# Retention attention and a low-rank mixer on one core: the third batch's k loaded and turned ahead of its q, and another order for the second batch's steps

## Chip, cores and metric

One core of one Trainium2 chip. The metric is the device time of one execution of the kernel in microseconds. The median of three runs before the change is 323.8 us (321.01 to 323.85).

## What is computed

The reference takes q, k and v (8 batches, 8 heads, 576 tokens, 64 channels) and four weight matrices. Cut to what matters:

```python
scores = scale * np.matmul(q, k.transpose(0, 1, 3, 2))
Dmat = np.where(rel >= 0, gamma[:, None, None] ** rel[None, :, :], 0.0)
attn = np.matmul(scores * Dmat[None], v)              # gamma = 1 - 2**(-5-head), rel = row - column
x = attn.transpose(0, 2, 1, 3).reshape(B, S, H * D)   # 8 x 576 x 512
h = x.transpose(0, 2, 1) @ U @ V                      # rank 32, over the tokens
u = x + h.transpose(0, 2, 1)
out = u + np.maximum(u @ w_ch1, 0.0) @ w_ch2          # 512 -> 2048 -> 512
```

## The kernel before

**Stages.** The 8 x 576 tokens make nine groups of 512 tokens for the MLP (j = 0 to 8). Attention and mixer work batch by batch. The first two batches (b = 0 and 1) run ahead of everything else in `early`; batch b = 2 runs inside the MLP units of group j = 1, and every later batch b inside group j = b - 1. All data are computed in bf16; a matmul accumulates in a PSUM bank, and another engine copies it out.

**The order in `early`.** The instructions of each engine run in the order in which the program issues them. For batches 0 and 1 that order stands in the string `EARLY` (lines 33 to 63), a list of steps separated by semicolons. `step` (line 631) issues the instructions of one step: the first number after the name is the batch, the second is the pair of heads, hp = 0 to 3, and what follows are the numbers of the PSUM banks that the step writes or the engine that does it. The names that are needed here, for a pair of heads of batch 1:

- `tk`, `tq`: PE turns k and q (transposes into a bank). `ck`: ACT copies the turned k into one of the two halves of `kvT` (`kT_bufs`, line 167). `qs`: DVE scales the turned q into `qz`.
- `sc`: PE forms the scores, into three banks. `ma`, `mb`, `ml`: DVE masks them into `ret`.
- `vs`: DVE scales v (from `v_given`, which lies in `kv_runs`) into `v_all`. `st`: PE sums the states, k times v. `S`: copies them out.
- `it`: PE multiplies the masked scores with v; `nt` adds the last block and q times the state. `xa`, `xb`: the result is copied into `x_t`.
- `dn`, `at`, `ux`, `uv`, `ua`, `ub`: the mixer and the turning of its sum u into `uT_t`.
- `M n`: PE runs unit n of the MLP of group 0, four matmuls of 128x512. Units 16 to 31 are the second product, four for each block of 128 tokens. They depend on nothing that batch 1 makes, and stand between its steps as filler. `O i`: DVE adds u to block i, and SP issues its store. `Y`, `Q`: the first three units of group 1, whose input is all of batch 1's u.
- `kt c`: SP issues a turn by DMA (`turn_by_dma`, line 475) of blocks c and c + 1 of batch 2's k, from `k_sets[2]` into `kT_sets`. `kT_sets[0]` is a tile of its own (`kT_all`), `kT_sets[1]` is the whole of `kvT`.

**Loads.** POOL issues the loads that convert from float32. In the step `hv` (`load_second_kv`, line 252) SP first loads parts of batch 1's k and all but one block of its v as float32; POOL casts the k of pairs 0 and 1 into `k_sets[1]`, scales one block of v, and calls `load_batch(2)` (line 304): four loads of q, then five blocks of k, then five of v. After `early` POOL issues `load_batch(3)`, with a scaling of v between the loads, and batch 3's q.

**Batches 2 and later.** `attention_steps` (line 560) puts steps at places among the MLP units. For b = 2 PE turns q (`psq`), k comes turned from `kT_sets`; DVE scales v (`scale_v`); `visit` runs state sums (`pss`), scores (`sc`), masks and the running state (`S`). From b = 3 on q and k are both turned by DMA, each batch's during the batch before it. Before the change batch b's k goes to `kT_sets[(b - NTURN) % 2]` with `NTURN` = 3, and batch 2's to `kT_sets[1]`, that is `kvT`, which batch 1's scores read until `sc 1 3`.

Of the kernel before, what the change touches and what calls it, by code (L numbers as in the profile page):

```python
# [14 lines left out]
class Pinned:  # L15
# [15 lines left out]


EARLY = """
    w 9; vs 0 1 POOL; lg; lw 0; lw 1; lw 2; lw 3; tk 0 0 0; w 4 4; tq 0 0 1; qs 0 0; ck
    0 0; bk 0 0 2; w 3 0; sc 0 0; vs 0 0 DVE; tk 0 1 3; mb 0 0; kk 0 0; ck 0 1; w 1 1;
    tq 0 1 4; st 0 0 0; ma 0 0; gv 0 2; it 0 0 1 2; qs 0 1; ml 0 0; S 0 0 ACT; bk 0 1 3;
    vl 0; gv 0 3; sc 0 1; exp 3; nt 0 0; mb 0 1; ma 0 1; kk 0 1; tk 0 2 4; tq 0 2 0; ml
    0 1; xa 0 0 ACT; qs 0 2; ck 0 2; tk 0 3 3; st 0 1 1; sc 0 2; S 0 1 ACT; it 0 1 4 0;
    ma 0 2; ck 0 3; mb 0 2; nt 0 1; tq 0 3 1; xb 0 0 ACT; bk 0 3 3; xa 0 1 ACT; bk 0 2
    2; ux 0 0 4; kk 0 2; xb 0 1 DVE; w 1 0; dn 0 0 0; ml 0 2; at 0 0 ACT; dn 0 1 2; at 0  # L40
    1 ACT; qs 0 3; vs 0 3 DVE; sc 0 3; vs 0 2 POOL; lw 4; lw 5; lw 6; lw 7; zm; l2; hk;
    st 0 2 1; kk 0 3; uv 0 0; ml 0 3; ma 0 3; mb 0 3; it 0 2 0 2; S 0 2 ACT; ua 0 0 ACT;
    st 0 3 3; nt 0 2; it 0 3 1 4; S 0 3 ACT; ux 0 1 3; xa 0 2 DVE; nt 0 3; xb 0 3 DVE;
    xb 0 2 ACT; dn 0 2 0; y 0 0; uv 0 1; xa 0 3 ACT; y 1 0; ux 0 2 2; at 0 2 DVE; y 2 0;
    dn 0 3 1; uv 0 2; ua 0 1 ACT; ux 0 3 4 0; at 0 3 ACT; ua 0 2 DVE; y 0 1; uv 0 3; y 1
    1; y 2 1; y 0 2; y 1 2; y 2 2; ub 0 3 DVE; ua 0 3 ACT; y 0 3; R 0; y 1 3; y 2 3; hu
    4 4; hu 2 0; R 1; ha 4; hu 1 2; hu 0 1; hu 3 3; R 2; M 3; ha 1; ha 2; M 4; R 3; z 3;
    exv; misc; hv; M 5; R 4; M 6; R 5; M 7; R 6; M 8; ha 0; R 7; ha 3; M 9; R 8; M 10; R
    9; M 11; R 10; M 12; R 11; M 13; R 12; M 14; R 13; M 15; R 14; M 16; R 15; M 17; M
    18; M 19; M 20; M 21; tq 1 0 0; qs 1 0; M 22; tk 1 0 1; tq 1 1 2; qs 1 1; ck 1 0; tk  # L50
    1 2 3; sc 1 0 4 0 1; M 23; mb 1 0; ml 1 0; tk 1 1 2; ma 1 0; vs 1 1 DVE; ck 1 2; ck
    1 1; M 24; tk 1 3 0; sc 1 1 3 1 4; M 25; M 26; ck 1 3; vs 1 0 DVE; st 1 1 2; ml 1 1; st 1
    0 4; S 1 1 ACT; ma 1 1; S 1 0 ACT; it 1 0 0 3; mb 1 1; it 1 1 2 1; nt 1 0; nt 1 1;
    vs 1 2 DVE; st 1 2 4; xa 1 0 ACT; xa 1 1 ACT; vs 1 3 DVE; xb 1 1 DVE; tq 1 2 0; tq 1
    3 2; xb 1 0 DVE; st 1 3 1; qs 1 2; qs 1 3; S 1 2 ACT; dn 1 0 4; O 0; sc 1 2 3
    0 2; at 1 0 DVE; mb 1 2; ml 1 2; S 1 3 ACT; ma 1 2; dn 1 1 1; M 27; sc 1 3 4 0 2; kt 0; kt 2; kt 4; M
    28; ux 1 1 3; at 1 1 ACT; ml 1 3; ma 1 3; mb 1 3; it 1 2 1 2; uv 1 1; M 29; it 1 3 4
    0; nt 1 2; ua 1 1 ACT; xb 1 2 DVE; O 1; nt 1 3; ux 1 0 3; xa 1 2 ACT; dn 1 2 1; xa 1
    3 ACT; at 1 2 DVE; uv 1 0; ux 1 2 2; xb 1 3 ACT; dn 1 3 4; uv 1 2; ua 1 0 ACT; O 2;
    at 1 3 DVE; ux 1 3 0 1; M 30; uv 1 3; ua 1 2 ACT; ua 1 3 ACT; ub 1 3 DVE; M 31; Y 0  # L60
    0; Y 0 1; Y 0 2; Y 0 3; Q 0; O 3; Y 2 0; Y 2 1; Y 2 2; Y 2 3; Q 2; Y 1 0; Y 1 1; Y 1
    2; Y 1 3; Q 1
"""


# [1 line left out]
def kernel(  # L67
# [72 lines left out]
    NRUNS = 3  # L140
    NTURN = 3
# [162 lines left out]
    def load_batch(b, blocks=range(NB)):  # L304

        if b < NRUNS:
            for hp in range(NHP):
                load_runs(in_runs(q_raw[b % NQ]), q, b, hp)
        elif blocks[0] == 0:
            m, pad = (NB - 1, slice(HALF, P)) if b % 2 == 0 else (0, slice(0, HALF))  # L310
            for x in (k_sets, v_sets):
                pool.memset(x[b % NSET][pad, m, :, :], 0.0)
        if b < NRUNS:
            for x, src in ((k_sets, k), (v_sets, v)):
                for m in blocks:
# [52 lines left out]
    def att_transposes(b, hp, st):  # L368
        if b < NRUNS:
            psq = turn_runs_by_head(in_runs(q_raw[b % NQ]), hp, "psq")  # L370
        elif b < NTURN:
            psq = turn_blocks(in_blocks(q_raw[b % NQ]), hp, "psq")
        else:
            psq = qT_sets[(b - NTURN) % 2][:, :, hp, :]
        st["qT"] = q_by_chunks(b, hp, psq)
        st["kT"] = kT_sets[(b - NTURN) % 2][:, :, hp, :]


    def q_by_chunks(b, hp, psq):
# [180 lines left out]
    def attention_steps(b, at, gap, at_mixer, at_turn=2):  # L560

        if b // 2 not in pairs:
            new_pair(b)
        pair = pairs[b // 2]
        x_t = work.tile([P, NB, dm], BF16, tag="x_t", name="x_t")
        sts = [{} for _ in range(NHP)]
        mst = {}
        steps = []

        for hp in range(NHP):  # L570
            if b < NRUNS:
# [25 lines left out]
    def early(mlp, mlp1, between):  # L597
# [33 lines left out]
        def step(op, args):  # L631
# [55 lines left out]
            if op == "lg":  # L687
                x = in_runs(k_raw)[:, H - 1, 0, 0:1]
# [25 lines left out]
            st, h, cols = sts[b, n], slice(2 * n, 2 * n + 2), slice(n * P, (n + 1) * P)  # L714
# [126 lines left out]
            elif op == "ux":  # L841
                k = (NB - 1) // len(i)
# [13 lines left out]
            elif op == "uv":  # L856
                k = (NB - 1) // len(st["u"])
# [19 lines left out]
        st = {"at": at_sb}  # L877
# [376 lines left out]
    while n < SP:  # L1254
        m = min(n, SP - n)
# [141 lines left out]
```

## Time and profile before

| | us |
|---|---|
| median of three runs | 323.8 |
| the three runs | 321.01, 323.80, 323.85 |
| the profiled execution's own time | 322.16 |
| its span, first to last instruction | 320.4 |
| PE busy | 310.9 |
| DVE busy | 231.4 |
| POOL busy | 158.9 |
| ACT busy | 149.5 |

The profiled execution's own time is 1.8 us longer than the span of its instructions. The granted TensorE clock is 1.00 throughout. PE, DVE, ACT, POOL and SP are TensorE, VectorE, ScalarE, GpSimd and SyncE; PEld is the weight load, which overlaps PE. A row of the profile names the output tile and the inputs, the shape, the number of instructions and, in brackets, the idle time of the engine before it with what ended it. All helpers record one line number, L25, so groups are told apart by their tiles: `ps_b` is a bank of `early`, `ps_y` the MLP, `pss` and `sc` the later batches' state sums and scores.

### The profile page before, as it was taken

The page shows a single profiled execution, that of the slowest core. Times are in us where ns is not written, and L with a number is a line of the kernel's source. Part 1 is how long each engine was busy: PE and PEld are TensorE (multiplying, and loading weights), DVE is VectorE, ACT ScalarE, POOL GpSimd, SP SyncE. Part 2 cuts the span into 40 slices and gives each one's busy share as a digit, 9 for nine tenths or more (in the row PEclk, how much of TensorE's full clock was granted, in tenths as well). Part 3 has the DMA queues.
Part 4 walks back from the last instruction along what each step waited for, and adds up shares of the span by engine and source line. Part 5 has one row for each costly group of instructions (what it writes and reads, how often), then busy time and mean ns, then how long its engine had stood idle before and what let it go on. Part 6 is the DMA issues. An engine that isn't in the chain of part 4 may idle for free.

```text
span 320.4 us, 9737 instructions
## 1 busy us (share of the span) xinstructions
PE 310.9 (97%) x4120; PEld 205.9 (64%) x4120; DVE 231.4 (72%) x552; ACT 149.5 (47%) x305; POOL 158.9 (50%) x197
## 2 busy tenths in 40 slices
PE   8999999999999999999999999999999999999995
PEld 3664446644544677845788878556867784585484
DVE  5977537749898998789878978897889772352244
ACT  7667523347620674067406750675067506604610
POOL 8582339948940998399649914650400040040040
PEclk9999999999999999999999999999999999999999
DMA  8999999999998999999999996994420043002003
GB/s 123 189 200 206 200 200 134 170 182 148 139 154 203 90 143 146 159 188 151 144 207 126 167 118 85 170 152 85 127 72 4 3 96 120 0 32 101 0 2 132
DMA packets 154524, 40.59 MB, mean 127 GB/s; under 512 B 139088, under 2 KB 153456, under 8 KB 154480
## 3 DMA queue, kind: packets, MB, share of 16 engines
q0 software_dynamic: 91344, 17.09, 68.9%
q1 hardware_dynamic: 63136, 22.88, 37.0%
q8 instruction: 32, 0.52, 0.7%
q14 instruction: 12, 0.10, 0.1%
HBM read 36.85 MB, written 9.44 MB: 144 GB/s over the span
## 4 chain that ended last, share of the span: by engine, by line
PE 64%; DVE 24%; DMA 6%; SPq 2%; issue 2%; POOL 0%; ACT 0%; DVEq 0%; POOLq 0%; ACTq 0%
PE ps_y L25 54%; DVE S L25 8%; DVE ret L25 7%; PE ps_b L25 4%; PE xh L25 3%; DMA kvT<-k_all 2%; DMA given<-in_v_dram 2%; DVE y_sums L25 2%; SPq L25 2%; DMA kv_runs<-in_v_dram 2%; DVE o_sb L25 2%; DVE kv_runs L25 1%; DVE u_t L25 1%; PE sc L25 1%; PE ps_h L25 1%
## 5 line engine op out<-in xcount | busy, mean ns | idle before, releaser
L25 PE MATMUL ps_y<-uT_t,w_sb 128*128 128x512 bf16 (+3 forms) x768 | 131.0, 326 | 0.0
L25 ACT ACTIVATE y_t<-ps_y 128x512 bf16<-128x512 f32 x144 | 85.5, 597 | 61.8 <-PE ps_y L25 60.7
L25 PEld LDWEIGHTS <-w_sb 128*128 128x128 bf16 x768 | 68.1, 98 | 50.4
L25 POOL TENSOR_TENSOR o_sb<-o_sb,u_t 128x512 f32<-128x512 f32 (+1 forms) x24 | 24.4, 1034 | 93.2 <-DVE o_sb L25 92.7
L25 PEld LDWEIGHTS <-y_t 128*128 128x128 bf16 x576 | 55.2, 98 | 18.0
L25 PE MATMUL ps_y<-w_sb,y_t 128*128 128x256 bf16 (+1 forms) x352 | 57.7, 311 | 0.0
L25 DVE SCALAR_TENSOR_TENSOR S<-S,keep,pss 128x64 bf16<-128x64 bf16 x168 | 46.9, 279 | 5.1
L25 DVE TENSOR_TENSOR o_sb<-ps_y,o_sb 128x512 f32<-128x512 f32 (+1 forms) x37 | 24.4, 662 | 26.5 <-PE ps_y L25 13.1
L25 DVE TENSOR_TENSOR ret<-sc,qsrow 128x640 bf16<-128x640 f32 x48 | 37.2, 816 | 7.2 <-PE sc L25 3.8
L25 POOL DMA_DIRECT2D k_all<-in_k_dram x36 | 30.9, 861 | 9.2 <-DMA w_sb<-in_moe_w_ch_dram 7.6
L25 PEld LDWEIGHTS <-y_sums 128*128 128x128 bf16 x336 | 32.0, 98 | 5.0
L25 POOL TENSOR_TENSOR v_all<-v_all,vs 128x512 bf16<-128x512 bf16 (+1 forms) x25 | 27.9, 1116 | 9.3 <-DMA v_all<-in_v_dram 8.8
L25 POOL DMA_DIRECT2D q_all<-in_q_dram x37 | 29.0, 796 | 4.2 <-DMA w_sb<-in_moe_w_ch_dram 4.2
L25 DVE TENSOR_TENSOR y_sums<-y_t 128x512 bf16<-128x512 bf16 x28 | 14.2, 508 | 22.1 <-ACT y_t L25 22.1
L25 PE MATMUL ps_y<-w_sb,y_sums 128*128 128x256 bf16 x224 | 27.3, 273 | 0.0
L25 PE MATMUL ps_y<-kv_runs,y_t 128*128 128x256 bf16 x224 | 27.1, 273 | 0.0
L25 POOL DMA_DIRECT2D v_all<-in_v_dram x31 | 26.8, 874 | 0.3 <-DMA q_all<-in_q_dram 0.3
L25 ACT CAST S<-pss 128x64 bf16<-128x64 f32 x24 | 5.1, 210 | 46.8 <-issue 41.4
L25 ACT ACTIVATE x_t<-xh,xs 128x320 bf16<-128x320 f32 x48 | 22.7, 524 | 7.0 <-PE xh L25 5.6
L25 DVE TENSOR_TENSOR u_t<-ps_h,x_t 128x512 bf16<-128x512 f32 (+1 forms) x35 | 22.3, 681 | 0.8 <-PE ps_h L25 0.4
L25 DVE TENSOR_TENSOR y_sums<-y_sums,y_t 128x512 bf16<-128x512 bf16 x28 | 14.2, 508 | 1.0
L25 POOL COPY landed<-uT_t 128x4 bf16<-128x4 bf16 (+1 forms) x4 | 0.8, 190 | 27.8 <-DMA uT_t<-u_t 27.8
(130 smaller groups left out, 313.8 us busy)
## 6 DMA issues: line engine op xcount, KB each, us to landing
out_dram<-o_sb SPq DMA_DIRECT2D x35, 256.0 KB, 2.9
w_sb<-in_moe_w_ch_dram POOLq DMA_DIRECT2D x8, 512.0 KB, 12.2
v_all<-in_v_dram POOLq DMA_DIRECT2D x25, 128.0 KB, 7.3
k_all<-in_k_dram POOLq DMA_DIRECT2D x24, 128.0 KB, 6.3
q_all<-in_q_dram POOLq DMA_DIRECT2D x20, 128.0 KB, 4.5
q_all<-in_q_dram POOLq DMA_DIRECT2D x12, 144.0 KB, 5.8
given<-in_v_dram SPq DMA_DIRECT2D x8, 128.0 KB, 4.2
kv_runs<-in_v_dram SPq DMA_DIRECT2D x3, 256.0 KB, 6.1
```

The source lines that it names most:

```text
L25: return self._tc.keep_in_program_order(call(*args, **kwargs))
```

## The change

In `EARLY` only batch 1's part differs, from `M 22` on. Cut to it, with the unchanged steps ahead of it left out:

```diff
-    ... M 21; tq 1 0 0; qs 1 0; M 22; tk 1 0 1; tq 1 1 2; qs 1 1; ck 1 0; tk
-    1 2 3; sc 1 0 4 0 1; M 23; mb 1 0; ml 1 0; tk 1 1 2; ma 1 0; vs 1 1 DVE; ck 1 2; ck
-    1 1; M 24; tk 1 3 0; sc 1 1 3 1 4; M 25; M 26; ck 1 3; vs 1 0 DVE; st 1 1 2; ml 1 1; st 1
-    0 4; S 1 1 ACT; ma 1 1; S 1 0 ACT; it 1 0 0 3; mb 1 1; it 1 1 2 1; nt 1 0; nt 1 1;
-    vs 1 2 DVE; st 1 2 4; xa 1 0 ACT; xa 1 1 ACT; vs 1 3 DVE; xb 1 1 DVE; tq 1 2 0; tq 1
-    3 2; xb 1 0 DVE; st 1 3 1; qs 1 2; qs 1 3; S 1 2 ACT; dn 1 0 4; O 0; sc 1 2 3
-    0 2; at 1 0 DVE; mb 1 2; ml 1 2; S 1 3 ACT; ma 1 2; dn 1 1 1; M 27; sc 1 3 4 0 2; kt 0; kt 2; kt 4; M
-    28; ux 1 1 3; at 1 1 ACT; ml 1 3; ma 1 3; mb 1 3; it 1 2 1 2; uv 1 1; M 29; it 1 3 4
-    0; nt 1 2; ua 1 1 ACT; xb 1 2 DVE; O 1; nt 1 3; ux 1 0 3; xa 1 2 ACT; dn 1 2 1; xa 1
-    3 ACT; at 1 2 DVE; uv 1 0; ux 1 2 2; xb 1 3 ACT; dn 1 3 4; uv 1 2; ua 1 0 ACT; O 2;
-    at 1 3 DVE; ux 1 3 0 1; M 30; uv 1 3; ua 1 2 ACT; ua 1 3 ACT; ub 1 3 DVE; M 31; Y 0
+    21; M 22; M 23; tq 1 0 0; tq 1 1 1; tk 1 0 2; M 24; tk 1 1 3; ck 1 0; qs 1 0; sc
+    1 0 4 0 2; qs 1 1; ma 1 0; mb 1 0; M 25; ck 1 1; sc 1 1 1 3 4; mb 1 1; M 26; tk
+    1 3 0; tk 1 2 3; ma 1 1; M 27; kt 0; kt 2; kt 4; vs 1 0 DVE; vs 1 1 DVE; ck 1 2;
+    ck 1 3; ml 1 0; st 1 0 1; st 1 1 3; it 1 0 0 2; ml 1 1; S 1 0 ACT; vs 1 3 DVE;
+    it 1 1 4 1; S 1 1 ACT; nt 1 0; nt 1 1; xb 1 0 ACT; xa 1 0 ACT; vs 1 2 DVE; O 0;
+    tq 1 2 3; st 1 2 2; qs 1 2; xb 1 1 ACT; xa 1 1 ACT; S 1 2 DVE; tq 1 3 0; st 1 3
+    1; sc 1 2 3 4 2; qs 1 3; S 1 3 ACT; ma 1 2; ml 1 2; dn 1 1 0; at 1 1 ACT; M 28;
+    sc 1 3 1 0 3; mb 1 2; ma 1 3; M 29; it 1 2 2 4; dn 1 0 1; at 1 0 ACT; mb 1 3; ml
+    1 3; nt 1 2; it 1 3 0 3; ux 1 1 1; nt 1 3; xa 1 2 ACT; uv 1 1; ux 1 0 2; O 2; xb
+    1 2 ACT; dn 1 2 4; xb 1 3 ACT; O 1; ua 1 1 ACT; xa 1 3 DVE; uv 1 0; dn 1 3 3; at
+    1 2 DVE; ux 1 2 0; ua 1 0 DVE; at 1 3 ACT; ux 1 3 1 4; uv 1 2; uv 1 3; M 30; M
+    31; ua 1 3 ACT; ua 1 2 DVE; ub 1 3 DVE; Y 0 0; ...
```

The loads of batch 2, and where turned k goes:

```diff
 def load_batch(b, blocks=range(NB)):
         if b < NRUNS:
+            for m in blocks:
+                load_block(k_sets[b % NSET], k, b, m)
             for hp in range(NHP):
                 load_runs(in_runs(q_raw[b % NQ]), q, b, hp)
-        elif blocks[0] == 0:
+            for m in blocks:
+                load_block(v_sets[b % NSET], v, b, m)
+            return
+        if blocks[0] == 0:
 ...
-        if b < NRUNS:
-            for x, src in ((k_sets, k), (v_sets, v)):
-                for m in blocks:
-                    load_block(x[b % NSET], src, b, m)
-            return
@@ att_transposes
-        st["kT"] = kT_sets[(b - NTURN) % 2][:, :, hp, :]
+        st["kT"] = kT_sets[b % 2][:, :, hp, :]
@@ attention_steps
-                                     (k_sets[(b + 1) % NSET], kT_sets[(b + 1 - NTURN) % 2]))):
+                                     (k_sets[(b + 1) % NSET], kT_sets[(b + 1) % 2]))):
@@ step
             if op == "kt":
-                turn_by_dma(k_sets[2], kT_sets[1], b)
+                turn_by_dma(k_sets[2], kT_sets[0], b)
```

So `M 22` and `M 23` now stand ahead of batch 1's first turn, and `M 27` ahead of its state sums; the masks `ma` and `mb` of pairs 0 and 1 ahead of the scaling of v on DVE; seven of the eight copies into `x_t` on ACT, where it was five; the three turns of batch 2's k ahead of `O 0`'s store on SP's queue, where they stood behind it, and into `kT_all`; and for every batch from 3 on the two buffers of turned k are exchanged.

More of the change, by code (lines that the diff above doesn't have):

```diff
@@ L33 @@
 EARLY = """
[L34 to L50, printed above, removed]
-    1 2 3; sc 1 0 4 0 1; M 23; mb 1 0; ml 1 0; tk 1 1 2; ma 1 0; vs 1 1 DVE; ck 1 2; ck
@@ L58 @@
-    0; nt 1 2; ua 1 1 ACT; xb 1 2 DVE; O 1; nt 1 3; ux 1 0 3; xa 1 2 ACT; dn 1 2 1; xa 1
-    3 ACT; at 1 2 DVE; uv 1 0; ux 1 2 2; xb 1 3 ACT; dn 1 3 4; uv 1 2; ua 1 0 ACT; O 2;
-    at 1 3 DVE; ux 1 3 0 1; M 30; uv 1 3; ua 1 2 ACT; ua 1 3 ACT; ub 1 3 DVE; M 31; Y 0
-    0; Y 0 1; Y 0 2; Y 0 3; Q 0; O 3; Y 2 0; Y 2 1; Y 2 2; Y 2 3; Q 2; Y 1 0; Y 1 1; Y 1
-    2; Y 1 3; Q 1
+    w 9; vs 0 1 POOL; lg; lw 0; lw 1; lw 2; lw 3; tk 0 0 0; w 4 4; tq 0 0 1; qs 0 0;
+    ck 0 0; bk 0 0 2; w 3 0; sc 0 0; vs 0 0 DVE; tk 0 1 3; mb 0 0; kk 0 0; ck 0 1; w
@@ new lines @@
+    1 1; tq 0 1 4; st 0 0 0; ma 0 0; gv 0 2; it 0 0 1 2; qs 0 1; ml 0 0; S 0 0 ACT;
+    bk 0 1 3; vl 0; gv 0 3; sc 0 1; exp 3; nt 0 0; mb 0 1; ma 0 1; kk 0 1; tk 0 2 4;
+    tq 0 2 0; ml 0 1; xa 0 0 ACT; qs 0 2; ck 0 2; tk 0 3 3; st 0 1 1; sc 0 2; S 0 1
+    ACT; it 0 1 4 0; ma 0 2; ck 0 3; mb 0 2; nt 0 1; tq 0 3 1; xb 0 0 ACT; bk 0 3 3;
+    xa 0 1 ACT; bk 0 2 2; ux 0 0 4; kk 0 2; xb 0 1 DVE; w 1 0; dn 0 0 0; ml 0 2; at
+    0 0 ACT; dn 0 1 2; at 0 1 ACT; qs 0 3; vs 0 3 DVE; sc 0 3; vs 0 2 POOL; lw 4; lw
@@ new lines @@
+    5; lw 6; lw 7; zm; l2; hk; st 0 2 1; kk 0 3; uv 0 0; ml 0 3; ma 0 3; mb 0 3; it
+    0 2 0 2; S 0 2 ACT; ua 0 0 ACT; st 0 3 3; nt 0 2; it 0 3 1 4; S 0 3 ACT; ux 0 1
+    3; xa 0 2 DVE; nt 0 3; xb 0 3 DVE; xb 0 2 ACT; dn 0 2 0; y 0 0; uv 0 1; xa 0 3
+    ACT; y 1 0; ux 0 2 2; at 0 2 DVE; y 2 0; dn 0 3 1; uv 0 2; ua 0 1 ACT; ux 0 3 4
+    0; at 0 3 ACT; ua 0 2 DVE; y 0 1; uv 0 3; y 1 1; y 2 1; y 0 2; y 1 2; y 2 2; ub
+    0 3 DVE; ua 0 3 ACT; y 0 3; R 0; y 1 3; y 2 3; hu 4 4; hu 2 0; R 1; ha 4; hu 1
@@ new lines @@
+    2; hu 0 1; hu 3 3; R 2; M 3; ha 1; ha 2; M 4; R 3; z 3; exv; misc; hv; M 5; R 4;
+    M 6; R 5; M 7; R 6; M 8; ha 0; R 7; ha 3; M 9; R 8; M 10; R 9; M 11; R 10; M 12;
+    R 11; M 13; R 12; M 14; R 13; M 15; R 14; M 16; R 15; M 17; M 18; M 19; M 20; M
+    21; M 22; M 23; tq 1 0 0; tq 1 1 1; tk 1 0 2; M 24; tk 1 1 3; ck 1 0; qs 1 0; sc
+    1 0 4 0 2; qs 1 1; ma 1 0; mb 1 0; M 25; ck 1 1; sc 1 1 1 3 4; mb 1 1; M 26; tk
+    1 3 0; tk 1 2 3; ma 1 1; M 27; kt 0; kt 2; kt 4; vs 1 0 DVE; vs 1 1 DVE; ck 1 2;
@@ L63 @@
+    1 2 ACT; dn 1 2 4; xb 1 3 ACT; O 1; ua 1 1 ACT; xa 1 3 DVE; uv 1 0; dn 1 3 3; at
+    1 2 DVE; ux 1 2 0; ua 1 0 DVE; at 1 3 ACT; ux 1 3 1 4; uv 1 2; uv 1 3; M 30; M
+    31; ua 1 3 ACT; ua 1 2 DVE; ub 1 3 DVE; Y 0 0; Y 0 1; Y 0 2; Y 0 3; Q 0; O 3; Y
+    2 0; Y 2 1; Y 2 2; Y 2 3; Q 2; Y 1 0; Y 1 1; Y 1 2; Y 1 3; Q 1
 """
```

## The prediction

> **What bounds the kernel now.** I read the page's busy table first, then the table of waits for who made TensorE (PE) stand idle, first from 42.4 to 71.6 us and then from there to the end.
>
> ```profile
> span 320.4 us, 9737 instructions
> ## 1 busy us (share of the span) xinstructions
> PE 310.9 (97%) x4120; PEld 205.9 (64%) x4120; DVE 231.4 (72%) x552; ACT 149.5 (47%) x305; POOL 158.9 (50%) x197
> ```
>
> ```profile
> PE sc L25 <- DMA kvT<-k_all: 0.7, 1, 0.7
> PE ps_b L25 <- POOL k_all L25: 0.6, 1, 0.6
> PE ps_b L25 <- DVE ret L25: 0.5, 2, 0.3
> PE ps_b L25 <- DVE qz L25: 0.3, 1, 0.3
> ```
>
> ```profile
> PE ps_ut L25 <- DVE u_t L25: 0.3, 1, 0.3
> PE xh L25 <- DVE o_sb L25: 0.2, 1, 0.2
> ```
>
> PE is the bound: 310.9 of 320.4 us. The change adds and removes no arithmetic, so it can win only what PE loses, and of that the stretch in which the second batch (batch 1) runs and batch 2 begins has 2.1 us; all of the 249 us behind it have 0.5. That stretch in PE's order of time (start, length, and in brackets the idle time before):
>
> ```profile
> 42.43 0.45 PE L25 MATMUL ps_b<-ident,q_all 96*64 96x96 bf16 x12
> 42.81 1.04 PE L25 MATMUL ps_y<-w_sb,y_t 128*128 128x512 bf16 x4
> 44.41 0.45 PE L25 MATMUL ps_b<-ident,k_all 128*128 128x128 bf16 x5 [0.57 <-POOL k_all L25]
> ...
> 50.88 0.51 PE L25 MATMUL ps_b<-v_all,k_all 128*64 128x64 bf16 x20
> ...
> 57.60 0.57 PE L25 MATMUL ps_b<-qz,kvT 64*128 64x128 bf16 x10
> 58.10 1.04 PE L25 MATMUL ps_y<-w_sb,y_t 128*128 128x512 bf16 x4
> ...
> 64.48 1.03 PE L25 MATMUL ps_y<-w_sb,y_t 128*128 128x512 bf16 x4
> 65.34 2.75 PE L25 MATMUL ps_y<-uT_t,w_sb 128*128 128x512 bf16 x12
> ...
> 70.23 0.32 PE L25 MATMUL pss<-v_all,k_all 64*64 64x64 bf16 x16
> 70.38 0.30 PE L25 MATMUL sc<-qz,kvT 64*64 64x64 bf16 x16
> 71.34 0.22 PE L25 MATMUL sc<-qz,kvT 64*64 64x64 bf16 x4 [0.66 <-DMA kvT<-k_all]
> ```
>
> The ends shown are modelled and overlap the next start, so I count from start to start. A unit of filler (M n, four matmuls) takes 64.48 to 65.34 = 0.86 us. M 22, at 42.81, was done at 43.67, so the k turn at 44.41 (tk 1 0) lost 0.74 us, not 0.57.
>
> This execution took 322.16 us; the median of the three runs is 323.8 (321.01 to 323.85), 1.64 more. I make the sum against 322.16 and scale it by 323.8/322.16. Less than about 1% a measurement of this kernel cannot tell from no change.
>
> **Part 1: the order of batch 1.** Two things feed it that the order does not move, the casts of k on POOL and the scaling of the landed v on VectorE (DVE):
>
> ```profile
> 43.64 0.72 POOL L25 CAST k_all<-y_sums 128x640 bf16<-128x640 f32 x1 [2.04 <-DMA y_sums<-in_k_dram]
> 44.87 0.72 POOL L25 CAST k_all<-y_sums 128x640 bf16<-128x640 f32 x1 [0.51 <-DMA y_sums<-in_k_dram]
> ```
>
> ```profile
> 50.11 1.29 DVE L25 TENSOR_TENSOR v_all<-kv_runs,vscale 128x512 bf16<-128x512 f32 x2 [2.53 <-DMA kv_runs<-in_v_dram]
> ```
>
> So k is cast at 44.36 (hp 0) and 45.59 (hp 1), and v of the first two pairs is scaled at about 50.75 and 51.40.
>
> In the new order M 22 and M 23 run from 42.43 to 44.15, and both q turns (0.38 each, 42.43 to 42.81) to 44.9. The turn of k hp 0 now comes after its cast and is over at 45.3, M 24 at 46.2, the turn of hp 1 at 46.5, after its cast too. Scores of hp 0 (0.50, 57.60 to 58.10), M 25, scores of hp 1, M 26, the turns for hp 3 and 2 and M 27 bring PE to about 50.7; the copies and masks between these steps lie beside an M each. There it meets the floor of v: the state sums of hp 0 start at about 50.8, where before those of hp 1 started at 50.88.
>
> So at that floor M 27 is done, where before M 26 was the last. From 50.88 to 65.34 were 14.46 us with five units; with four they are 13.60, and from 50.8 PE comes to batch 2's MLP units at 64.4 if the other waits stay as they were: **0.95 us** won.
>
> The waits after the floor are the term I know least. The table marks 0.8 of them (0.5 on ret, 0.3 on qz); start to start, where modelled ends hide part, I read up to 1.5. Walking the new order with the same lengths I find four: v of hp 1, 0.2 (51.4 against 51.2); dn 1 1, whose bank is freed by a q copy queued on DVE behind O 0 and S 1 2, 0.5; it 1 3 for its last mask, 0.25; small ones 0.1. That is 1.05 against 1.5, a gain of 0.4; adding the steps' own lengths alone I end at 63.5, a gain of 0.9. If one bank comes free a DVE operation later than I read it, 0.5 is lost instead. Range -0.5 to 0.9; I take **0.6**, between my two readings. The masks now stand ahead of the v scaling on DVE, which idled 2.53 us there, so nothing is held up by that; the copies of x_t move from DVE to ACT, which was busy 47% of the span.
>
> **Part 2: batch 2's k ahead of its q, and turned at once.** POOL's issues, the k loads' times to landing, the turns on SP's queue with theirs, and the v loads with the median of theirs:
>
> ```profile
> 48.65 2.58 POOL L25 DMA_DIRECT2D q_all<-in_q_dram  x4
> 51.22 4.22 POOL L25 DMA_DIRECT2D k_all<-in_k_dram  x5
> 55.38 4.25 POOL L25 DMA_DIRECT2D v_all<-in_v_dram  x5
> ```
>
> ```profile
> DMA to landing us min/median/max: 5.1/5.5/5.9
> ```
>
> ```profile
> L25 SPq DMA_TRANSPOSE kvT<-k_all x3: 1342/1382/3958, 58.3 to 63.8; - x3
> ...
> DMA to landing us min/median/max: 7.5/8.8/10.2
> ```
>
> ```profile
> v_all<-in_v_dram POOLq DMA_DIRECT2D x4, 128.0 KB, 6.3
> out_dram<-o_sb SPq DMA_DIRECT2D x1, 256.0 KB, 4.6
> v_all<-in_v_dram POOLq DMA_DIRECT2D x1, 64.0 KB, 8.0
> ```
>
> The first turn was issued at 58.3, just after hp 3's scores (57.60 to 58.10) had read kvT for the last time. It now writes kT_all, which nobody reads, and waits for its two k blocks alone. The k issues move up by 2.57 us, so these land at about 54.5, and the turns go out at about 55, 57 and, with the 5.5 us from first to last as before, at most 60.5. With 7.5 to 10.2 to land, the last is there by 68 to 70 and more likely at 68; its chunk was wanted at 70.68 (71.34 less 0.66) and will be at 69.1. The wait goes: **0.7**, and 0 if it stayed.
>
> What this is moved past: O 0's store stands behind the turns on SP's queue, and waits with them; O 0 to O 3 have a buffer each, so nobody waits for that store. q is issued from 52.9 to 55.4, lands by about 61 and is turned on PE after 66. Batch 3's k is turned into kvT, free since 58.2. v is issued at the same times, since the same nine transfers stand before it.
>
> The cover that can go is v's. Its last block, issued at about 58.9, landed 8.0 later, at 66.9, and DVE scaled v at 67.23:
>
> ```profile
> 67.23 1.55 DVE L25 TENSOR_TENSOR v_all<-v_all,vs 128x640 bf16<-128x640 bf16 x2
> 72.03 1.55 DVE L25 TENSOR_TENSOR ret<-sc,qsrow 128x640 bf16<-128x640 f32 x2 [3.25 <-ACT S L25]
> ```
>
> PE's state sums (70.23) need hp 0's half, 0.78 after v. PE 1.55 us earlier wants them at 68.7, so v by 67.9: 1.0 us of room. Of the turns' 13.0 us (58.3 to 71.3) the last 4.4 lay behind v's landing; now that third shares the transfers with v. v comes 0 us later if the transfers have room for both, 2.2 if they share evenly, and that costs PE 0 to 1.2. I charge **-0.3**, nearer to 0: an even share of half of that third already fits the room.
>
> **The sum.** 0.95 + 0.6 + 0.7 - 0.3 = 1.95 us. Behind 72 us PE waits only 0.5 us in all, each time for an engine whose work moves up with PE, and DVE idles 3.25 us before its next block, so I carry the gain to the end: 322.16 - 1.95 = 320.2, which is 321.8 in terms of the median.
>
> **Rivals.** *A, more is won.* The runs at 323.8 may be executions in which the k turns landed 1.64 us later still (their times to landing differ by 2.7). There the removed wait is 1.64 longer, v's charge is not paid, and 1.95 + 1.64 + 0.3 are won: 319.9. For it: that wait is PE's longest in the stretch; against: no trace shows those runs.
>
> *B, v takes the place of kT.* v comes 2.2 late and costs 0.9 more than charged: 1.05 is won, 322.7. For it: room of only 1.0, and v's time to landing, which had grown from 6.3 to 8.0 beside the turns; against: the turns then ran beside batch 3's loads as well.
> The Trainium skill (DMA: Bandwidth & Descriptors, Issuing engines are not separate DMA queues) says that transfers issued by SP and by POOL run on the same 16 engines and interleave, which speaks against turning early and for B. The trace agrees as far as that growth of 1.7 us goes.
>
> *C, slower.* The turns push v behind them altogether, so that v's last block lands at 71.3, where the turns ended before. Scaling hp 0 then ends at 72.1, and the state sums, which without the kT wait could have started at 70.9 before (70.23 + 0.66), start 1.2 us late: 323.4, or 325.0 in the median. It decides from v landing at 70.1, 3.2 later than before. For it: v stands behind k and q in one queue; against: two thirds of the turns delayed v by only 1.7.
>
> **How the numbers follow.** Forecast 0.50, A 0.20, B 0.18, C 0.12. Faster by over 1% (below 320.6): A, and the upper end of the forecast, 0.26. Slower by over 1% (above 327.0): C with 2 us more, 0.05. Within 1%: 0.69. The forecast's own range is 320.6 (0.9 for 0.6, 0.7 and no charge, and the median's scatter) to 323.2 (-0.5 for 0.6, and 0.3 more of charge). To 8 in 10 it takes in B and the larger part of A, and half of C: 319.4 to 324.4.
>
> **What would show it.** No PE wait for POOL's cast; state sums of hp 0 at 50.8; batch 2's first MLP unit near 63.8 instead of 65.34; the turns issued from about 55 and no PE wait for kT; the scaling of v at 67 to 68 and batch 2's state sums near 68.7. It would be wrong if PE stood idle before those sums for v, if the turns were issued no earlier than 58, if the new order held PE more than 1.6 us after 50.8, or if the gain were lost at the start of the third MLP group, where PE reads batch 2's turned u.

## The result, and the profile after

| | before | after |
|---|---|---|
| median, us (20 runs each) | 321.32 | 325.89 |
| lowest and highest, us | 319.60, 323.85 | 322.63, 328.86 |
| ratio to before, 95% interval | | 1.0117 [1.0092, 1.0143] |
| the profiled execution's own time, us | 322.16 | 327.08 |

The ratios are taken over undisturbed runs alone, so they can differ a little from the quotient of the medians. The change made the kernel slower by 1.2%. It was predicted at 321.8 (319.4 to 324.4); the time lies above that range, and a loss came where a gain was forecast. The twenty runs also put the median before at 321.32, not at the 323.8 of the three runs that the forecast was scaled to.

The busy table of after, with its row of the granted clock over the span:

```profile
span 325.4 us, 9740 instructions
PE 311.6 (96%) x4120; PEld 206.2 (63%) x4120; DVE 232.7 (72%) x551; ACT 149.0 (46%) x306; POOL 158.6 (49%) x197
...
PEclk9999999996999999999999999999999999999999
```

PE's work is the same, and the span is 4.94 us longer (325.36 against 320.42). One slice, the tenth (73.2 to 81.4 us), was granted clearly less than the others. The table of waits for PE (us in total, times, longest; its first five rows) names the place:

```profile
PE pss L25 <- DVE v_all L25: 5.2, 1, 5.2
PE ps_warm L25 <- DVE warm L25: 1.1, 1, 1.1
PE ps_b L25 <- POOL v_all L25: 0.6, 1, 0.6
PE ps_y L25 <- DMA uT_t<-u_t: 0.6, 1, 0.6
PE ps_b L25 <- DVE qz L25: 0.3, 1, 0.3
...
```

The waits for `kvT`, for POOL's cast of k and for `ret` are gone. In their place stands one of 5.2 us at batch 2's state sums. (The 0.6 for POOL's `v_all` is at 14.0 us, in batch 0, which the change doesn't touch; from there comes the late start of batch 1 below.) PE's order of time in that stretch:

```profile
64.18 2.75 PE L25 MATMUL ps_y<-uT_t,w_sb 128*128 128x512 bf16 x12
66.86 0.45 PE L25 MATMUL psq<-ident,q_all 96*64 96x96 bf16 x12
67.24 1.90 PE L25 MATMUL ps_y<-uT_t,w_sb 128*128 128x512 bf16 x8
74.31 0.43 PE L25 MATMUL pss<-v_all,k_all 64*64 64x64 bf16 x16 [5.17 <-DVE v_all L25]
74.50 0.51 PE L25 MATMUL sc<-qz,kT_all 64*64 64x64 bf16 x20
74.94 3.60 PE L25 MATMUL ps_y<-uT_t,w_sb 128*128 128x512 bf16 x8
78.47 0.49 PE L25 MATMUL psq<-ident,q_all 96*64 96x96 bf16 x12
78.89 1.90 PE L25 MATMUL ps_y<-uT_t,w_sb 128*128 128x512 bf16 x8
80.72 0.32 PE L25 MATMUL xh<-S,qz 64*64 64x64 bf16 x16
80.87 0.30 PE L25 MATMUL pss<-v_all,k_all 64*64 64x64 bf16 x16
```

Eight MLP matmuls take 1.90 us at 67.24 and 3.60 at 74.94: just behind the wait PE runs at half speed. The chain of waits of after, cut to what leads to those sums (start, length, what), shows who is late:

```profile
58.67 0.86 POOL v_all L25
59.54 13.67 DMA v_all<-in_v_dram
...
73.43 0.84 DVE v_all L25
74.27 0.04 issue
74.31 0.43 PE pss L25 x15
```

The last block of v, issued at 59.54, landed 13.7 us later, at 73.21. Before it had taken 8.0, to 66.86. Of the 6.35 us between the two landings, 0.68 is the later issue (59.54 against 58.86) and 5.67 the longer transfer.

The 4.94 us from start to start, where before has batch 2's first sums at 70.23 and its second (pair 1's) at 75.73. The order puts two MLP units (1.72) ahead of batch 1's first turn, so after's 44.59 stands for 42.87:

| stretch | before | after | difference |
|---|---|---|---|
| start to batch 1 | 42.43 | 42.87 | +0.44 |
| batch 1, to batch 2's first MLP unit (65.34; 64.18) | 22.91 | 21.31 | -1.60 |
| to its first state sums | 4.89 | 10.13 | +5.24 |
| to its second state sums | 5.50 | 6.56 | +1.06 |
| the rest of the span | 244.69 | 244.49 | -0.20 |

### The profile page after: what moved, and what is told of

Same layout as the page of the kernel before. It is cut to its first block, busy times and chain, and to the rows that moved or that the text cites. A ratio compares the mean times of both kernels' runs of the same rounds, so it can differ in the third digit from the quotient of the medians.

```text
span 325.4 us, 9740 instructions
## 1 busy us (share of the span) xinstructions
PE 311.6 (96%) x4120; PEld 206.2 (63%) x4120; DVE 232.7 (72%) x551; ACT 149.0 (46%) x306; POOL 158.6 (49%) x197
## 4 chain that ended last, share of the span: by engine, by line
PE 54%; DVE 21%; DMA 16%; POOL 6%; issue 2%; SPq 0%; DVEq 0%; POOLq 0%
PE ps_y L25 47%; DVE S L25 8%; DVE ret L25 6%; DMA v_all<-in_v_dram 6%; DMA w_sb<-in_moe_w_ch_dram 6%; PE xh L25 3%; DVE y_sums L25 3%; DMA given<-in_v_dram 2%; POOL v_all L25 2%; POOL k_all L25 2%; DMA uT_t<-u_t 2%; POOL w_sb L25 1%; DVE o_sb L25 1%; PE ps_h L25 1%; POOL q_all L25 1%
## 5 line engine op out<-in xcount | busy, mean ns | idle before, releaser
L25 PE MATMUL ps_y<-uT_t,w_sb 128*128 128x512 bf16 (+3 forms) x768 | 132.7, 329 | 0.6 <-DMA uT_t<-u_t 0.6
L25 DVE TENSOR_TENSOR y_sums<-y_t 128x512 bf16<-128x512 bf16 x28 | 15.2, 544 | 22.1 <-ACT y_t L25 22.1
L25 PEld LDWEIGHTS <-k_all 64*64 64x64 bf16 (+2 forms) x564 | 10.3, 110 | 9.1 <-issue 8.1
```

The source lines that it names most:

```text
L25: return self._tc.keep_in_program_order(call(*args, **kwargs))
```

## The experiments

**What was to be told apart.** Theory: the early turns take the transfers from v. Rival for the slowness: the new order. Rival for v's lateness: that q now stands right ahead of v in POOL's queue. The table of all runs comes first; the second and third columns come from the DMA issues in the traces. "Turn against v" is the issue of the first turn less that of the first block of v. Both columns come from one trace of each kernel. Where two traces have the same loads and turns, v's last block differs by 0.4 us (after and e4_pe_busy) and by 0.8 (e3_q_first and e11_q_first_again).

| kernel | loads | turn against v, us | last v block, issue to landing, us | ratio to before [95%] |
|---|---|---|---|---|
| before | q, k, v | +2.9 | 8.0 | |
| after | k, q, v | -1.4 | 13.7 | 1.0117 [1.0092, 1.0143] |
| e1_order_only | q, k, v | +3.1 | 8.8 | 1.0037 [1.0005, 1.0070] |
| e2_turns_only | k, q, v | -1.2 | 12.5 | 1.0066 [1.0018, 1.0114] |
| e3_q_first | q, k, v | +2.4 | 6.9 | 0.9967 [0.9938, 0.9995] |
| e4_pe_busy | k, q, v | -1.8 | 14.1 | 1.0061 [1.0028, 1.0093] |
| e5_k_first_late_turns | k, q, v | +2.0 | 10.9 | 1.0056 [1.0014, 1.0098] |
| e6_q_last | k, v, q | +2.2 | 7.0 | 1.0027 [0.9984, 1.0070] |
| e7_stores_later | k, q, v | -1.3 | 11.1 | 1.0294 [1.0197, 1.0390] |
| e8_other_buffer | q, k, v | +2.9 | 8.3 | 0.9992 [0.9956, 1.0028] |
| e9_turns_after_v | k, q, v | +8.6 | 4.7 | 1.0114 [1.0062, 1.0167] |
| e10_no_turns | k, q, v | none | 7.4 | 0.9935 [0.9901, 0.9969] |
| e11_q_first_again | q, k, v | +2.9 | 7.7 | 0.9962 [0.9930, 0.9993] |
| e12_turns_after_v1 | k, q, v | +6.8 | 5.0 | 1.0026 [0.9988, 1.0065] |

### The order alone, the turns alone

Of after, e1_order_only keeps only the new order; loads and buffer are those of before, and the turns stand where `kvT` is free again (of its edit, the part in `EARLY`):

```diff
-    ... M 27; kt 0; kt 2; kt 4; vs 1 0 DVE; ...    sc 1 3 1 0 3; mb 1 2; ...
+    ... M 27; vs 1 0 DVE; ...    sc 1 3 1 0 3; kt 0; kt 2; kt 4; mb 1 2; ...
```

> Part 1 alone: the new order of batch 1's steps, with the loads of batch 2 as before (q, k, v), its turned k in kvT again and the three turns behind the scores of hp 3 as before. Theory (the order wins, the early turns lose): the front gain of 1.2 to 1.9 us shows at batch 2's first MLP unit, about half of it is lost again to the wait for kT, which is ready no earlier than before (0.7 becomes 1.5 to 2.0), so 0.3 to 1.0 us faster than before, and v is there by 67. Rival (the new order itself is what makes it slower): 3 us or more slower than before.

e2_turns_only has the order of before with the other two parts, loads k, q, v and the turns early into `kT_all` (of its edit against before, the part in `EARLY`):

```diff
-    ... M 25; M 26; ck 1 3; ...    sc 1 3 4 0 2; kt 0; kt 2; kt 4; M 28; ...
+    ... M 25; M 26; kt 0; kt 2; kt 4; ck 1 3; ...    sc 1 3 4 0 2; M 28; ...
```

> Part 2 alone: batch 1's steps in the order of before, with batch 2's k read in front of its q and turned as soon as it lands into kT_all (the three turns stand where M 26 ends). Theory (turns in flight hold back the loads of v): v's last block lands at 71 to 74, PE waits 2 to 4 us before batch 2's state sums, 3 to 6 us slower than before with the clock that falls after such a wait. Rival (the new order alone is at fault): no wait for v over 0.5 us, within 0.7 us of before.

Measured: e1_order_only took 322.99 us beside 321.35 of before, ratio 1.0037. e2_turns_only has a ratio of 1.0066 [1.0018, 1.0114], 2.1 us. In e1_order_only the new order brings PE to batch 2's first MLP unit at 63.80, with batch 1 begun 0.74 late (44.89 less 1.72, against 42.43): 2.3 us won there. The time is not shorter all the same. The waits for PE in e1_order_only begin with

```profile
PE sc L25 <- DMA kvT<-k_all: 1.7, 2, 1.1
```

so 1.0 of it went back to turned k, which lands as late as before (70.97 against 71.30) while PE wants it sooner. The second state sums start at 75.35, 0.4 ahead of before; yet the span is 0.9 longer and the ratio 1.2 us over before, and no wait in the profile accounts for that. It stays open. The order alone doesn't slow the kernel by after's 3.8 us: the rival falls.

In e2_turns_only the last v block takes 12.5 us instead of 8.0, with before's order, and PE waits for it:

```profile
PE pss L25 <- DVE v_all L25: 1.6, 1, 1.6
```

The wait is shorter than after's because PE comes later (at 69.8, where after came at 69.14) and v lands sooner (70.28, where after's landed at 73.21). Part 2 alone makes v late.

### Where q stands

e3_q_first is after with one thing put back: q is loaded ahead of k again. The turns still go early into `kT_all`.

```diff
         if b < NRUNS:
-            for m in blocks:
-                load_block(k_sets[b % NSET], k, b, m)
             for hp in range(NHP):
                 load_runs(in_runs(q_raw[b % NQ]), q, b, hp)
-            for m in blocks:
-                load_block(v_sets[b % NSET], v, b, m)
+            for x, src in ((k_sets, k), (v_sets, v)):
+                for m in blocks:
+                    load_block(x[b % NSET], src, b, m)
             return
```

> The changed kernel with the loads of batch 2 in the old order (q, k, v); the turns still go to kT_all as soon as k lands, which is now some 2.5 us later. Theory (the turns hold back v wherever they lie beside it): the first turn is issued at about 57, v's last block lands at 70 to 73 and PE still waits 1.5 to 4 us for it. Rival (it is the place of q between k and v that makes v late): v lands by 67.5, no wait for v over 0.5 us, 1 to 2.5 us faster than before.

Measured: 320.27 us, ratio 0.9967 [0.9938, 0.9995]. My theory had v still late, and it was not: the last block took 6.9 us, and batch 2's state sums follow the MLP without a wait. PE's order of time in e3_q_first:

```profile
63.12 2.75 PE L25 MATMUL ps_y<-uT_t,w_sb 128*128 128x512 bf16 x12
...
66.19 1.90 PE L25 MATMUL ps_y<-uT_t,w_sb 128*128 128x512 bf16 x8
68.02 0.32 PE L25 MATMUL pss<-v_all,k_all 64*64 64x64 bf16 x16
68.16 0.66 PE L25 MATMUL sc<-qz,kT_all 64*64 64x64 bf16 x20
68.75 1.90 PE L25 MATMUL ps_y<-uT_t,w_sb 128*128 128x512 bf16 x8
```

The turns wait for k, and with k second they were issued at 57.06 instead of 54.47, behind the first loads of v (54.62) and not ahead of them. So "turned early" had two halves, q's place and the turns' start. The next runs part them.

e5_k_first_late_turns keeps q between k and v and issues the turns late (the order as in e1_order_only, into `kvT`; of its edit, the part in `EARLY`):

```diff
-    ... M 27; kt 0; kt 2; kt 4; vs 1 0 DVE; ...    sc 1 3 1 0 3; mb 1 2; ...
+    ... M 27; vs 1 0 DVE; ...    sc 1 3 1 0 3; kt 0; kt 2; kt 4; mb 1 2; ...
```

> The changed kernel with batch 2's k still read first, but turned into kvT, so that the turns wait for the scores of hp 3 and start at about 57.5 instead of 52.7 to 54.5. Theory (v is late because the turns are in flight before v's loads begin): v's last block lands by 68.5, no wait for v over 0.7 us, a wait for kT of 1 to 2 us, the time of the order alone (323.0) within 1 us. Rival (reading k in front of q is itself what makes v late): v lands at 70 or later and the time stays at 325 to 326.

e6_q_last puts q behind v:

```diff
         if b < NRUNS:
             for m in blocks:
                 load_block(k_sets[b % NSET], k, b, m)
-            for hp in range(NHP):
-                load_runs(in_runs(q_raw[b % NQ]), q, b, hp)
             for m in blocks:
                 load_block(v_sets[b % NSET], v, b, m)
+            for hp in range(NHP):
+                load_runs(in_runs(q_raw[b % NQ]), q, b, hp)
             return
```

> The changed kernel with batch 2 read in the order k, v, q; the turns still start as soon as k lands, at about 53 to 55. Theory (turns in flight before v's loads hold v back): v is issued 2.5 us earlier but most of it still lands beside the turns, its last block at 66 to 70, and q, now behind, lands at 68 to 72, after PE wants it at 66: a wait of 2 to 5 us for q or v, slower than before by 1 to 5 us. Rival (q between k and v takes the room that v needs): v lands by 64, q by 67, at least as fast as the fastest so far (320.3).

e10_no_turns leaves the three turns of batch 2's k out. Its turned k is set to zero, so that batch 2's scores are zero:

```diff
-    1 3 0; tk 1 2 3; ma 1 1; M 27; kt 0; kt 2; kt 4; vs 1 0 DVE; vs 1 1 DVE; ck 1 2;
+    1 3 0; tk 1 2 3; ma 1 1; M 27; vs 1 0 DVE; vs 1 1 DVE; ck 1 2;
...
+        dve.memset(kT_sets[0], 0.0)
```

> The changed kernel without the three turns of batch 2's k: kT_all is set to zero instead, so batch 2's scores are zero and its output is wrong in that part. It prices the turns as a whole. Theory: v's last block lands at 60.5 to 63, PE waits for nothing before batch 2's state sums, and the time is that of the fastest so far or a little less (318 to 320.3). Rival (something else than the turns is slow in that stretch, such as POOL's issue or the stores): v at 66 or later and 322 or more.

Measured in v's last block: 10.9 us in e5_k_first_late_turns (PE waits 2.1 for v and 0.4 for `kvT`), 7.0 in e6_q_last, 7.4 in e10_no_turns, all beside 13.7 in after. Without turns, q between k and v costs nothing that shows beside before's 8.0 (7.4, landed at 64.86, where 60.5 to 63 was expected), and turns in flight beside v cost little with q out of the way (6.9, 7.0, 7.7). Together they cost 6. Neither the theory nor its rival was whole: v is late when the turns start while q, and v behind it, are still in POOL's queue. A later start alone does not keep them apart: with the turns 2.0 us behind v's first issue half of the delay was still there. e1_order_only and e5_k_first_late_turns differ in q's place alone (8.8 and 10.9 us), so with late turns that place costs 2.1. No run has the turns issued ahead of v with q out of the way, so what the early start costs by itself isn't shown.

e6_q_last gained nothing in time (322.77 beside 321.73 of before, ratio 1.0027). q landed at 66.5 and PE did not wait for it, but later it waited 1.5 us for a transfer of `uT_t`; its profiled span, 319.8, is shorter than before's while its median is not, and I can't say why.

### The clock behind the wait

e4_pe_busy is after with 20 matmuls of 128x512 on `warm` ahead of batch 2's first state sums, into a bank that nobody reads; PE works through the wait.

```diff
+        if b == 2 and n == 0:
+            ps = ps_mm.tile([P, 4, P], FP32, tag="mm", name="ps_fill")
+            for _ in range(20):
+                pe.matmul(
+                    ps, warm, warm[:, None, :].to_broadcast([P, 4, P]), start=True, stop=True
+                )
```

> The changed kernel with 20 matmuls of 128x512 on a constant tile in front of batch 2's first state sums, whose result nobody reads; they take 4.3 us at full clock and lie in the wait for v. Theory (after the wait PE works 6.8 us at half clock, and that is 3.4 us of the loss): the clock stays at 1.00, v lands as late as before, and the time is 2.5 to 3.5 us shorter than the changed kernel's, 0.5 us slower to 1 us faster than the kernel before. Rival (the low clock costs nothing, since other engines set the pace there): the same time as the changed kernel, or longer where its wait is shorter than the added work.

Busy time in four stretches (us; PE, PEld, DVE, ACT, POOL; then the granted clock, the DMA share and GB/s), in after:

```profile
64.00:69.00 5.00, 5.00 (x34) 2.15 (x32) 1.77 (x9) 2.92 (x5) 1.41 (x3) 1.00 1.33 153
69.00:72.00 3.00, 0.14 (x1) 0.10 (x1) 0.00 (x0) 0.60 (x1) 0.72 (x1) 0.96 1.55 278
72.00:78.00 6.00, 3.69 (x44) 1.61 (x43) 4.32 (x9) 0.81 (x2) 4.59 (x5) 0.50 2.04 132
78.00:82.00 4.00, 4.00 (x87) 2.06 (x86) 2.00 (x5) 2.80 (x6) 3.99 (x5) 0.92 1.51 96
```

and in e4_pe_busy:

```profile
69.00:72.00 3.00, 3.00 (x16) 1.35 (x14) 0.00 (x0) 0.00 (x0) 0.56 (x1) 1.00 1.93 219
72.00:78.00 6.00, 5.28 (x107) 2.52 (x108) 5.44 (x12) 2.75 (x6) 4.79 (x6) 1.00 1.93 125
```

With PE busy the clock stays at 1.00. From the first to the second state sums it takes 4.60 us (73.22 to 77.82) instead of 6.56: the halved clock costs 1.96. By the ratios it is 1.0117 less 1.0061, 0.56% or 1.8 us, somewhat under the expectation; the two intervals just touch, so the size is rough. v is as late as in after (14.1 us for its last block); I put the rest of the slowdown down to the wait itself.

### The stores, the buffer, and turns held back

e7_stores_later takes group 0's four stores out of SP's queue, where they stand behind the turns, and lets ACT issue them among group 1's units:

```diff
+    stores = []
...
-            sp.dma_start(out=out.rearrange("b s d -> (b s) d")[t0:t0 + P, :], in_=o_sb)
+            if j == 0:
+                stores.append(lambda: put(act))
+            else:
+                put(sp)
...
+                + [(9.2 + i, 6, s) for i, s in enumerate(stores)]
```

> The changed kernel with the four stores of the first MLP group issued from ScalarE among the second group's units, at about 74 to 78, instead of from SyncE behind the turns at 60.6 to 65.1. Theory (the turns alone hold v back; the stores behind them only add): v's last block lands 2 to 4 us sooner than in the changed kernel, at 69 to 71, PE waits 1 to 3 us instead of 5.2, and the clock does not fall or falls for less time: 2 to 4 us faster than the changed kernel, still not faster than the kernel before. Rival (the stores are what holds v back): v lands by 68 and the time is 319 to 320.5. Third (the stores do not matter): v lands at 72 to 73 as before and the time stays within 1 us of 325.9.

Measured: v's last block took 11.1 us, 2.6 less than in after, and landed at 69.75; PE's wait before the sums fell to 2.3. So after's stores, issued from 60.6 on and landed from 69.2 to 71.8, seem to have taken part of v's time too. It is one trace, of a long execution (336.56 us; the shortest took 330.54). The time, 333.22, says nothing of v: behind v's landing, from 80.0 us on, ACT stood still for 10.5 us between its second store and its third, and PE waited 10.0 for ACT. The trace puts the end of it down to a turn of batch 3's q; why the third store waited was not looked into.

```profile
ACT y_t L25 <- DMA qT_all<-q_all: 10.5, 1, 10.5
```

e8_other_buffer is before with the turns early into `kT_all`, loads in before's order:

```diff
-    ... M 26; ck 1 3; ...    sc 1 3 4 0 2; kt 0; kt 2; kt 4; M 28; ...
+    ... M 26; kt 0; kt 2; kt 4; ck 1 3; ...    sc 1 3 4 0 2; M 28; ...
-                turn_by_dma(k_sets[2], kT_sets[1], b)
+                turn_by_dma(k_sets[2], kT_sets[0], b)
```

> The kernel before with only the other buffer: batch 2's loads in the order q, k, v and batch 1's steps as before, but the turns go to kT_all and stand where M 26 ends, so that they start when k lands, at about 57 instead of 58.3. Theory (a start of the turns at about 57 is early enough for kT and late enough for v): the turns land by 69.5, PE's wait for kT (0.7) goes, v lands by 67.5: 0.3 to 1.2 us faster than before. Rival (turns in front of v cost v whatever their start): a wait for v of 1 us or more, not faster than before.

Measured: 321.72 against 321.73 of before; the expected gain did not come. The turns leave no earlier against v (+2.9 us, as before), since they wait for k, and PE still waits 0.6 us for `kT_all`. The other buffer alone is worth nothing that can be told (ratio 0.9992, within 0.4%).

e9_turns_after_v and e12_turns_after_v1 are after with the turns held back: POOL writes a padding row of `k_sets[2]` from the last block of v (from block 1 in e12_turns_after_v1), and the turn that reads this row is issued first.

```diff
+        pool.tensor_scalar(
+            out=k_sets[2][HALF:P, NB - 1, 0, 0:1], in0=v_sets[2][0:HALF, NB - 1, 0, 0:1],
+            scalar1=0.0, scalar2=None, op0=ALU.mult,
+        )
...
-    ... M 27; kt 0; kt 2; kt 4; ...
+    ... M 27; kt 4; kt 0; kt 2; ...
```

> The changed kernel (loads k, q, v; turns into kT_all) with the turns and batch 3's loads held until v's last block has landed, by one small GpSimd operation that reads it; block 4 is turned first. Theory (v is late because the turns begin before v's loads are through): v's last block lands at 61 to 63.5 instead of 73, no PE wait for v; the turns start at 62 to 64 and land at 69 to 72, so that PE waits 0 to 3 us for kT; 2.5 to 5 us faster than the changed kernel. Rival (reading k in front of q makes v late by itself): v lands at 66 or later although no turn is in flight.

> The changed kernel (loads k, q, v; turns into kT_all), with the turns held only until the second of v's five blocks has landed, by the same small GpSimd operation reading that block instead of the last. Theory (it is the start of the turns against v's loads that decides, not the place of k in front of q): the turns start at 60 to 62, v's last block lands at 62 to 66, PE waits for v not at all and for kT 0 to 2 us, and the time is 319.5 to 322, at least 3.5 us less than the changed kernel's. Rival (with k in front of q the stretch stays slow whenever the turns start): 324 or more.

Measured: v's last block took 4.7 and 5.0 us, the shortest of all, and no PE wait for batch 2's v is left. These two runs hold back more than the turns: POOL's queue stands with them, so batch 3's first load is issued at 63.8 or later instead of 61.14, and SP's stores, behind the turns, at 67.2 or later instead of 60.63. That may be why v is quicker here than in e10_no_turns (7.4), and they don't price the turns alone. In e9_turns_after_v the time didn't follow (325.17, four runs). Its profile lost about 3 us before 24 us, ahead of anything that the edit touches: group 0's first MLP unit starts at 24.26 instead of 21.32 in after and 20.89 in before, behind a stretch of halved clock from 14.5 to 17.9. Whether its other runs did the same isn't known, so its time is left open. e12_turns_after_v1 came to 322.67 beside 320.95 of before; by the ratios (1.0117 less 1.0026) that is 2.9 us under after, as the theory had it in sign, short of the 3.5 expected. It gained nothing over before, and a wait for the turns stands where the wait for v was. Waits for PE in e12_turns_after_v1:

```profile
PE sc L25 <- DMA kT_all<-k_all: 2.6, 1, 2.6
```

The turns land at 65.40, 68.36 and 72.27, and PE wants the last at 69.7. Late turns free v and are late themselves.

e11_q_first_again is the kernel of e3_q_first in five rounds, since its gain is near what can be told.

> The version with q in front of k, the early turns into kT_all and the new order once more, in five rounds, to tell whether it is faster than the kernel before. Expected 0.3 to 0.9% faster; the rival is that the first three rounds were luck and it is the same within 0.2%.

Measured: 320.54 against 321.61, ratio 0.9962 [0.9930, 0.9993]. Here PE waits 1.3 us for `kT_all` in the profile, and the span is still 1.9 us under before's. It is the one version, with all three turns in it, that beats both kernels: the new order and the other buffer, without k ahead of q.

## Why the prediction was wrong

**The order of batch 1 (right, and closer than its grounds).** Predicted: 0.95 + 0.6 = 1.55 us won by batch 2's first MLP unit. The trace has 1.60 (21.31 against 22.91). The wait for POOL's cast is gone. But the old order, too, has no such wait in e2_turns_only and e8_other_buffer, and its three traces took 22.91, 22.55 and 21.66 for this stretch. A gain is borne out, since no trace with the new order took over 21.39; that it came within 0.05 us of the sum is luck. The state sums of hp 0, expected at 50.8, start at 51.37; 0.44 of that is the late start, which leaves 0.1. Against the trace of before, the other runs with this order show 1.5 to 2.3 at the same place (e11_q_first_again to e1_order_only).

**The turns and the wait for kT (right).** Predicted: issued at about 55, 57 and at most 60.5, the last landed more likely at 68, and 0.7 us saved. Measured: 54.47, 56.97, 58.74, the last landed at 68.44, no wait. PE, held up by v, came for turned k only at 74.50, so the missing wait proves little; but 68.44 would have been early enough for the 69.1 forecast. v's first issue, said to be unchanged, moved from 55.38 to 55.85, as much as the whole stretch.

**v (the step that failed).** "v comes 0 us later if the transfers have room for both, 2.2 if they share evenly, and that costs PE 0 to 1.2. I charge -0.3." v came 6.35 us later (73.21 against 66.86), and PE's first state sums 5.24 later after the first unit. The term was mis-sized for two reasons. It counted only the last third of the turns as new beside v, since two thirds had overlapped v before. But before they met a queue in which q was through (its last load landed at 55.67, the first turn left at 58.25); now all three met it with q and v still to come. q itself, forecast to land by about 61, landed at 63.21. And it looked at O 0's store alone, and put that at no cost because nobody waits for it. SP's issues, before and after:

```profile
56.75 0.36 SPq L25 DMA_DIRECT2D out_dram<-o_sb  x1
58.25 6.88 SPq L25 DMA_TRANSPOSE kvT<-k_all  x3
65.23 1.49 SPq L25 DMA_DIRECT2D out_dram<-o_sb  x3
```

```profile
54.47 6.07 SPq L25 DMA_TRANSPOSE kT_all<-k_all  x3
60.63 4.80 SPq L25 DMA_DIRECT2D out_dram<-o_sb  x4
```

Before, three of the four stores stood behind the long issue of the turns and landed from 72.1 us on, behind v's last block. With the turns earlier, all four were issued from 60.6 to 65.1 and landed ahead of v's last block. e7_stores_later, without them there, had that block 2.6 us quicker. What each kind of transfer got, from 54 to 70 us (packets, MB, share of 16 engines), before:

```profile
DMA packets 14943, 2.58 MB, mean 161 GB/s; under 512 B 14617, under 2 KB 14813, under 8 KB 14941
...
q0 software_dynamic: 12404, 1.68, 170.3%
q1 hardware_dynamic: 2537, 0.86, 38.0%
```

and after:

```profile
DMA packets 8658, 2.58 MB, mean 161 GB/s; under 512 B 7546, under 2 KB 8314, under 8 KB 8656
...
q0 software_dynamic: 5626, 1.19, 101.0%
q1 hardware_dynamic: 3030, 1.36, 62.1%
```

The same 2.58 MB moved. SP's queue (q1: turns and stores) took 0.50 MB more of them, and POOL's loads (q0) 0.49 less. The Trainium skill (DMA: Bandwidth & Descriptors, Issuing engines are not separate DMA queues) says that transfers of all issuers run on the same engines and interleave. The trace agrees in so far as the share by bytes turned from 34% for SP's queue (0.86 of 2.54 MB) to 53% (1.36 of 2.55). The prediction had cited it for rival B, and then priced a sharing by duration.

The sizes of the packets tell whose bytes these are. A store of 256 KB is 128 packets of 2 KB. Of these (from 2 to 8 KB in the first line) there were 128 before and 342 after, 0.44 of the 0.50 MB. A load of q, 144 KB, is 192 packets of 768 B. Of these (from 512 B to 2 KB) there were 196 before and 768 after, 0.44 MB more. The turns moved about as much as before in these 16 us (0.66 MB, 0.60 before).

But they moved it while v was queued. From 58 to 66 us, ahead of the packets of after's stores, the turns moved 0.49 MB in after, 0.37 in before and none in e10_no_turns. POOL's loads moved 0.54, 0.71 and 1.02, of which q's took 0.30, none and 0.08. Turns and loads together come to 1.0 to 1.1 MB in all three: what the turns and q moved, k and v didn't (0.24 MB in after, 0.71 before, 0.94 in e10_no_turns). Then, from 66 to 70 us, the stores moved 0.70 MB and POOL's loads 0.12.

**The rivals.** B had the wait at the right place, but at 2.2 us late. C had the mechanism, the turns pushing v behind them, with v at 71.3 and 1.2 us for PE; v landed 1.9 later still. C, with its chance of 0.12, came nearest (325.0 in the median, where 325.89 was measured). C set it against two thirds of the turns having delayed v "by only 1.7", and that row was taken with q out of the way: e5_k_first_late_turns beside e1_order_only, and e6_q_last beside after, show that q's place matters to what the turns cost v.

**The clock (not foreseen).** PE stood idle and then ran at a granted clock of 0.50: 1.06 us more to the second state sums, although the wait for kT in that stretch had gone. Nothing in the profile of before, whose clock is 1.00 throughout, showed that a PE wait could cost more than its length.

The sum: 4.94 us more where 1.95 less were forecast, 6.9 apart. Of it 4.9 is v (5.24 for 0.3), 1.7 the clock (1.06 and the 0.66 of kT that it hid; e4_pe_busy puts it at 1.96), 0.4 the start, which is no part of the change (batch 0's v landed 0.4 later in this trace), less 0.2 in the rest.

**Still open:** why e1_order_only lost 1.3 us behind 75 us; the times of e6_q_last and e9_turns_after_v; how much of v's delay each of the 256 KB stores makes, since only moving all four was tried; and what the turns' early start costs v by itself.

## What to carry to other kernels

A transfer that is moved earlier is paid by whatever is still queued beside it at the new time: list those transfers, who needs them first and by when, and count the stores or loads that the move pushes into the same stretch, before crediting the wait that it removes. Take the slowdown of a transfer only from a stretch with the same queue beside it; a row from a stretch where q was already through (1.7 us) gave less than a third of what it cost here, 5.7. Where a new PE wait of some us is possible, price the clock behind it as well.

## What the hardware showed that was not expected

**The clock.** After's PE was idle from 69.14; the trace has its granted clock at 0.50 from 71.78, 2.6 us into the wait, for 6.83 us, 4.3 of them with PE at work again. In e5_k_first_late_turns waits of 2.1 and 0.4 us were followed by 3.4 us at 0.50; in e12_turns_after_v1 a single wait of 2.6 was not:

```profile
69.00:72.00 3.00, 0.70 (x26) 0.27 (x24) 0.00 (x0) 0.86 (x3) 2.72 (x3) 1.00 1.96 168
72.00:78.00 6.00, 5.69 (x105) 3.05 (x106) 4.72 (x11) 3.46 (x8) 2.82 (x3) 1.00 1.84 240
```

The length of the idle time alone does not decide. All changes of the granted clock lie a whole number of steps of 3.41 us from the first one of their trace, in all fourteen traces (in after 19, 21 and 93 steps, in e5_k_first_late_turns 20, 21 and 93). So where an idle time falls on these steps may matter. But in the step that ends where the halving begins PE stood idle for 2.64 us in after, 1.89 in e5_k_first_late_turns and 1.25 in e9_turns_after_v, and in e12_turns_after_v1 for 1.84 without any halving; what decides stays open. The Trainium skill (TensorE: Matmul & The Clock Gate, What's actually happening) has half rate after at least one idle window of about 3.4 us, counted by a window that runs freely; the steps here agree with such a window, and the halving after 2.64 us or less of idle time in a step is earlier than the figure.

**Stretches in which hardly anything moved.** The row of GB/s in after, 40 slices of 54 to 70 us (0.4 us each):

```profile
GB/s 142 187 138 121 139 146 144 173 168 175 119 136 109 96 172 222 184 142 142 158 155 141 166 147 79 6 10 118 154 154 158 93 19 120 280 343 310 316 341 333
```

At 64.0 to 64.8 us 6 and 10 GB/s moved, with all of v, two of the turns and three of the stores still out. Other runs have such gaps too (12 GB/s in a slice of e2_turns_only). What causes them was not tried.
